# Swapping the row halves of odd heads so that the value products use all four 64x64 tiles of TensorE

## The chip, the cores and the metric

The kernel runs on one core of a Trainium2 chip. The metric is the device time of one execution in microseconds. A core has TensorE (PE in the profile, with its weight loads listed apart as PEld), VectorE (DVE), ScalarE (ACT), GpSimd (POOL) and a queue that issues transfers (SP).

## What is computed

An mLSTM cell over 4 batches x 8 heads (32 heads, called BH), 768 steps and 40 channels, and behind it a feed-forward block over the 3072 tokens. Cut to what matters:

```python
for t in range(S):                       # S = 768, for each of the 32 heads
    m_new = maximum(f_gate[t] + m, i_gate[t])
    f_stab, i_stab = exp(f_gate[t] + m - m_new), exp(i_gate[t] - m_new)
    C = f_stab * C + i_stab * outer(v[t], k[t])        # 40 x 40
    n = f_stab * n + i_stab * k[t]
    y[t] = sigmoid(o_gate[t]) * (C @ q[t]) / maximum(abs(n @ q[t]), 1)
h = y.reshape(3072, 320) @ w_in                        # 320 -> 2048
out = (h * sigmoid(1.702 * h)) @ w_out                 # 2048 -> 320
```

## The kernel before

The 768 steps are cut into six windows `w` of L = 128 steps, for all four batches at once (512 tokens a window). In a window the recurrence is written as attention: within the window a masked 128 x 128 matrix of scores times decay weights is multiplied with the values, and what came before the window enters through a state matrix per head. The normaliser `n` is carried as a column of ones beside the 40 channels of the values (`D1` = 41).

Window 0 is done whole at the start. Windows 1 to 5 are cut in two halves of HL = 64 steps, `x` = 0 and 1. Only the two diagonal 64 x 64 blocks of the scores are then needed; what the first half gives to the second goes through a state in the middle, `state_mid`. All of it is done in two calls `c` = 0 and 1 of 16 heads (PH), eight pairs (NJ) of an even head `i` = 0 and an odd head `i` = 1. For one such window:

- `gates` (DVE) runs two scans over the gates of all heads (rows of 32 partitions) and leaves `st`, 96 rows x 128 steps: rows 0-31 hold the gate term of the keys, rows 32-63 the decay of the queries, rows 64-95 the decay of the values to the end of their half. `m_row` sends the running maximum to memory.
- `spread` fetches `m_row` back, repeated over 64 partitions, into `wt` (steps of keys on partitions, pair, head of the pair, 64 steps of queries).
- `columns` (L288) transposes `st` on PE, so that steps stand on partitions, and the results `cols` are exponentiated by ACT.
- `weights` (L346) makes the decay weights from `wt` and a column of `cols` on ACT, POOL masks them (L350).
- `scores` (L370) multiplies keys with queries in 64 x 64 blocks into the two banks of one PSUM tile, and DVE multiplies the result into `wt` (L373).
- `values` multiplies `wt` with the values (p_o, L411) and the queries with the two states (p_i, L421). DVE adds the two parts (L428, L429), and `outputs` divides and gates.
- `seam` (L438) transposes the result for the feed-forward block, `scale` and `carry` (L464) make the new states.

For a product, the partitions of its two operands name the rows of PE's array, and the partitions of its output name the columns; with 64 on both sides there are four such tiles. In `scores` head `i` stands on rows 64 `i`, and half `x` goes to columns 64 `x`, so all four tiles occur. In `values` the keys' steps are the rows and the queries' steps are the columns, and both come from the same half `x`, so that only the two tiles on the diagonal occur, one bank for each:

```python
for x in range(2):
    t, i = slice(x * HL, x * HL + HL), x ^ flip
    T.matmul(po[t, i, j * D1:(j + 1) * D1], wt[w, c][t, j, i, :], v_st[t, c * PH + 2 * j + i, :],
```

`within(0)` runs the even head of half 0 and the odd head of half 1, then come the products with the states, then `within(1)` the rest.

The order of the work is written out by hand. A window's feed-forward block has an up stage, whose products alternate with DVE, ACT and POOL work and in which the next window's gates, loads and spread are placed, and a down stage of 14 blocks (16 in window 0). `attention` hangs the next window's steps behind given blocks of the down stage: the columns behind block 0, the two calls of `weights` behind 1 and 2, `carry` behind 4, `scores` behind 6, `values` behind 7 and 8, the transposes of `seam` behind 9 and 11 (window 1: 0, 1, 3, 4, 8, 9, 10, 11, 13). Each engine runs its instructions in that order. PSUM tiles of two banks (`banks`: p_cols, p_s, p_o, p_i, p_c, p_x and one of the up stage) share two slots in turn. All transfers go through SP's queue in the order of the program.

Of the kernel before, what the change touches and what calls it, by code (L numbers as in the profile page):

```python
# [26 lines left out]
def kernel(  # L27
# [81 lines left out]
    def load(w, what, bs=slice(0, B)):  # L109
        hs = slice(bs.start * H, bs.stop * H)  # L110
        for c in what:
            if c == "o" and w not in eo:
                eo[w] = ld.tile([L, BH, D], FP, tag="eo", bufs=1, name="eo")
            dst, src = {"k": (k_of(w), k), "q": (q_st, q), "v": (v_st, v), "o": (eo.get(w), o_gate)}[c]
            nc.sync.dma_start(out=dst[:, hs, 0:D],
                              in_=src[bs, :, w * L:(w + 1) * L, :].rearrange("b h s d -> s (b h) d"))

# [80 lines left out]
    for j in range(3):  # L198
        V.tensor_scalar(out=pick[j * BH:(j + 1) * BH, :], in0=ident[0:BH, 0:BH], scalar1=-1.0, scalar2=None,
                        op0=OP.mult)  # L200

    half = const.tile([BH, 2, 64], FP, name="half")
    par = const.tile([BH, 2], FP, name="par")
    pair = const.tile([BH, BH // 2], FP, name="pair")
# [27 lines left out]

    def gates(w):
        m = m_at[w]
        f_run = gate.tile([BH, L], FP, bufs=1, name="f_run")
        m_run = gate.tile([BH, L], FP, bufs=1, name="m_run")
        st = stacked[w] = gate.tile([3 * BH, L], FP, bufs=1, name="st")
        V.tensor_tensor_scan(out=f_run, data0=ones, data1=f_sb[w], initial=0.0, op0=OP.mult, op1=OP.add)
        a = st[0:BH, :]
        V.tensor_tensor(out=a, in0=i_sb[w], in1=f_run, op=OP.subtract)  # L240
        if w == 0:
            room = work.tile([L, H, D1], FP, tag="u", name="room").rearrange("p h d -> p (h d)")
            neg, part = room[0:BH, 0:L], room.bitcast(BF)[0:BH, 2 * L:3 * L]
            V.tensor_tensor(out=neg, in0=f_run, in1=i_sb[w], op=OP.subtract)
            for j in range(3):
                G.tensor_copy(out=part, in_=neg)
                G.tensor_copy(out=a3[j * BH:(j + 1) * BH, :], in_=part)
                if j < 2:
                    G.tensor_tensor(out=neg, in0=neg, in1=part, op=OP.subtract)
        V.tensor_tensor_scan(out=m_run, data0=ones, data1=a, initial=m, op0=OP.mult, op1=OP.max)  # L250
        if w == 0:

            room = work.tile([L, H, D1], FP, tag="u", name="room").rearrange("p h d -> p (h d)")
            left, part = room[0:BH, 0:L], room.bitcast(BF)[0:BH, 2 * L:3 * L]
            for j in range(3):
                rest = left if j else m_run
                V.tensor_copy(out=part, in_=rest)
                V.tensor_copy(out=m3[j * BH:(j + 1) * BH, :], in_=part)
                if j < 2:
                    V.tensor_tensor(out=left, in0=rest, in1=part, op=OP.subtract)  # L260
        else:
            m_row[w] = rows.tile([BH, L], FP, name="m_row")
            nc.sync.dma_start(out=m_row[w], in_=m_run)
        end = m_run[:, L - 1:L]
        if w + 1 < NW:
            m_at[w + 1] = gate.tile([BH, 1], FP, name="m_end")
            V.tensor_tensor(out=m_at[w + 1], in0=f_run[:, L - 1:L], in1=end, op=OP.add)

        mid = m_run[:, HL - 1:HL]
        for x, (old, new) in enumerate(((m, mid), (mid, end)) if w else ((m, end),)):  # L270
            t = slice(x * HL, x * HL + HL) if w else slice(0, L)
            V.tensor_scalar(out=st[BH:2 * BH, t], in0=m_run[:, t], scalar1=old, scalar2=None, op0=OP.subtract)
            V.tensor_scalar(out=st[2 * BH:3 * BH, t], in0=a[:, t], scalar1=new, scalar2=-1.0, op0=OP.subtract,
                            op1=OP.mult)
        if w:
            dec[w] = gate.tile([BH, 2, BH // 2], FP, name="dec")
            both = gate.tile([BH, 2], FP, name="both")
            V.tensor_tensor(out=both[:, 0:1], in0=m, in1=mid, op=OP.subtract)
            V.tensor_tensor(out=both[:, 1:2], in0=mid, in1=end, op=OP.subtract)
            for x in range(2):  # L280
                V.tensor_scalar(out=dec[w][:, x, :], in0=pair, scalar1=both[:, x:x + 1], scalar2=None, op0=OP.mult)

    def banks(name):
        return ps_a.tile([128, 2, 512], FP, tag="a", name=name)

    def columns(w):
        pt = banks("p_cols")[:, 0, :]
        T.transpose(pt[:, 0:3 * BH], stacked[w], ident[0:3 * BH, 0:3 * BH])  # L288
        n = 3 * BH
        if w in dec:  # L290
            n += BH
            T.matmul(pt[:, 3 * BH:n], half.rearrange("p a b -> p (a b)"), dec[w].rearrange("p a b -> p (a b)"),
                     start=True, stop=True)
        c = cols[w] = gate.tile([L, 4 * BH], FP, name="cols")
        V.tensor_copy(out=c[:, 0:BH], in_=pt[:, 0:BH])
# [25 lines left out]
    def spread(w):  # L321

        for c in range(2):
            x = wt[w, c] = work.tile([L, NJ, 2, HL], FP, tag="wt", bufs=2, name="wt")
            for i in range(2):
                src = m_row[w][c * PH:(c + 1) * PH, i * HL:(i + 1) * HL]
                nc.sync.dma_start(out=x[i * HL:(i + 1) * HL].rearrange("s j i t -> s (j i) t"),
                                  in_=src.unsqueeze(0).to_broadcast([HL, PH, HL]))

    def weights(w, c):  # L330
        if w == 0:
# [21 lines left out]
    def scores(w, c):  # L353
        if w == 0:
            pw = [ps_m.tile([L, NP, L], FP, tag="m", name="p_s") for _ in range(2)]
            for p in range(NP):
                for i in range(2):
                    r = slice(i * 64, i * 64 + D)
                    T.matmul(pw[i][:, p, :], kT[w, c][r, p, :], qT[w, c][r, p, :], start=True, stop=True)  # L359
            for i in range(2):  # L360
                V.tensor_tensor(out=wt[w, c][:, :, i, :], in0=pw[i], in1=wt[w, c][:, :, i, :], op=OP.mult)  # L361
            return
        pw = banks("p_s")
        for j in range(NJ):
            b, p = 2 * c + j // NP, j % NP
            for i in range(2):
                r = slice(i * 64, i * 64 + D)
                for x in range(2):
                    t = slice(x * HL, x * HL + HL)
                    T.matmul(pw[t, i, j * HL:(j + 1) * HL], kT[w, b][r, p, t], qT[w, b][r, p, t], start=True,  # L370
                             stop=True)
# [22 lines left out]
    def values(w, c):  # L394
# [9 lines left out]
        hs = slice(c * PH, (c + 1) * PH)  # L404
        po, pi = banks("p_o"), banks("p_i")

        def within(flip):
            for j in range(NJ):
                for x in range(2):
                    t, i = slice(x * HL, x * HL + HL), x ^ flip  # L410
                    T.matmul(po[t, i, j * D1:(j + 1) * D1], wt[w, c][t, j, i, :], v_st[t, c * PH + 2 * j + i, :],  # L411
                             start=True, stop=True)

        within(0)
        for j in range(NJ):
            b, p = 2 * c + j // NP, j % NP
            for i in range(2):
                r = slice(i * 64, i * 64 + D)
                for x, s in enumerate((state[w % 2], state_mid)):
                    t = slice(x * HL, x * HL + HL)  # L420
                    T.matmul(pi[t, i, j * D1:(j + 1) * D1], qT[w, b][r, p, t], s[r, c * NJ + j, :], start=True,  # L421
                             stop=True)
# [34 lines left out]
    def carry(w, c):  # L457
        js = slice(c * NJ, (c + 1) * NJ)
        pc = banks("p_c")
        halves = [slice(0, L)] if w == 0 else [slice(x * HL, x * HL + HL) for x in range(2 if w + 1 < NW else 1)]  # L460
        for j in range(NJ):
            for i in range(2):
                for x, t in enumerate(halves):
                    T.matmul(pc[i * 64:i * 64 + 64, x, j * D1:(j + 1) * D1], k_cols(w, t, c * PH + 2 * j + i),  # L464
                             vw[w, c][t, 2 * j + i, :], start=True, stop=True)
# [4 lines left out]
        for x, dst in enumerate((state_mid, state[1 - w % 2])[:len(halves)]):  # L470
# [346 lines left out]
```

## Time and profile before

| | |
|---|---|
| time, median of 3 runs | 494.53 us (494.53 to 494.54) |
| span of the profile | 492.8 us |
| PE busy | 485.8 us (99%), granted clock 1.000 |
| PEld / DVE / ACT / POOL busy | 394.4 / 343.5 / 194.5 / 149.7 us |
| p_o of windows 1 to 5 (L411) | 640 records, mean 228 ns |
| p_i (L421) | 640 records, mean 228 ns |
| columns (L288) | 6 records, mean 257 ns |
| spread (`wt<-m_row`) | 20 transfers of 256 KB, 6.2 us to landing |
| values (`v_st<-in_v_dram`), keys (`k_st<-in_k_dram`) | 640 KB each, 13.5 and 10.2 us to landing |

A record is one pass of a matmul through the array; a float32 product has two. The mean length of a record says nothing on how fast they follow one another, since many are under way at a time: for that, the chain of waits and the timeline give when a group starts and when the next one does. The chain names a group by line with the time from its start to the start of the next; some records can be missing from a count. "issue" is time in which an engine waited for nothing that the profile shows.

### The profile page before, as it was taken

How to read it: one execution, taken by the hardware profiler on the slowest of the kernel's cores; microseconds unless marked ns; L12 is line 12 of the kernel's file. 1: busy time of each engine (PE TensorE's matmuls, PEld its weight loads, DVE VectorE, ACT ScalarE, POOL GpSimd, SP SyncE). 2: the span in 40 equal slices, each digit the busy share in tenths (PEclk: the TensorE clock that was granted, in tenths of full speed). 3: DMA queues.
4: the chain of work that ended last, by engine and by line, in shares of the span. 5: the costliest groups of instructions: out<-in, count | busy, mean ns of one | idle time of the engine just before them, and what ended most of it. 6: DMA issues, size and time to landing. Idle time of an engine off the chain costs nothing.

```text
span 492.8 us, 11991 instructions
## 1 busy us (share of the span) xinstructions
PE 485.8 (99%) x4996; PEld 394.4 (80%) x4996; DVE 343.5 (70%) x668; ACT 194.5 (39%) x432; POOL 149.7 (30%) x145
## 2 busy tenths in 40 slices
PE   8989999999999999999999999999999999999997
PEld 5764447787777999767999877999876999876997
DVE  5776786977778965768966668967567957353812
ACT  4655558701454801444800354720164630164200
POOL 6020004300497700127610136620045640035300
PEclk9999999999999999999999999999999999999999
DMA  7789997006990000999000899000699000000000
GB/s 164 151 239 180 255 212 177 2 17 118 203 180 4 3 29 3 172 192 127 3 29 3 147 193 151 1 31 3 118 198 171 3 29 3 28 1 1 0 28 27
DMA packets 130342, 44.31 MB, mean 90 GB/s; under 512 B 105168, under 2 KB 127728, under 8 KB 130288
## 3 DMA queue, kind: packets, MB, share of 16 engines
q1 hardware_dynamic: 130288, 43.54, 49.6%
q8 instruction: 39, 0.64, 0.6%
q14 instruction: 15, 0.12, 0.1%
HBM read 39.52 MB, written 4.01 MB: 88 GB/s over the span
## 4 chain that ended last, share of the span: by engine, by line
PE 95%; DVE 3%; POOL 1%; ACT 0%; issue 0%; POOLq 0%; DVEq 0%
PE p_out L658 32%; PE p_h L556 25%; PE p_h L561 8%; PE p_out L607 7%; PE p_h L486 6%; PE p_o L411 4%; PE p_c L464 2%; PE p_s L370 2%; PE p_i L421 2%; PE p_h L492 2%; PE p_x L438 1%; PE p_t L310 1%; PE p_o L401 1%; PE p_s L359 0%; DVE wt L361 0%
## 5 line engine op out<-in xcount | busy, mean ns | idle before, releaser
L598 POOL TENSOR_TENSOR g<-g,parts 128x512 f32<-128x512 f32 x30 | 38.3, 1275 | 128.6 <-DVE parts L590 117.5
L658 PE MATMUL p_out<-w_out_sb,g 128*128 128x160 f32 x480 | 71.0, 302 | 0.0
L658 PEld LDWEIGHTS p_out<-w_out_sb,g 128*128 128x128 f32 x480 | 66.5, 190 | 0.9
L556 PE MATMUL p_h<-xT,w_in_sb 128*128 128x256 f32 x240 | 66.9, 388 | 0.0
L537 ACT ACTIVATE g<-g 128x512 f32<-128x512 f32 x80 | 49.6, 630 | 34.3 <-DVE g L593 25.2
L556 PEld LDWEIGHTS p_h<-xT,w_in_sb 128*128 128x128 f32 x240 | 43.7, 190 | 20.2 <-issue 7.6
L440 ACT COPY xT<-p_x 128x768 f32<-128x768 f32 (+1 forms) x14 | 9.9, 707 | 120.8 <-PE p_x L438 120.8
L663 DVE TENSOR_TENSOR o_sb<-o_sb,p_out 128x160 f32<-128x160 f32 x70 | 21.0, 316 | 46.0 <-PE p_out L658 45.6
L658 PE MATMUL p_out<-t_sb,s 128*128 128x160 f32 x320 | 47.1, 300 | 0.0
L658 PEld LDWEIGHTS p_out<-t_sb,s 128*128 128x128 f32 x320 | 44.4, 190 | 0.2
L589 DVE TENSOR_TENSOR t_x<-p_h,parts 128x256 f32<-128x256 f32 x40 | 16.8, 420 | 39.3 <-PE p_h L561 34.3
L556 PE MATMUL p_h<-t_x,s_in 128*128 128x256 f32 x160 | 41.1, 379 | 0.0
L561 PE MATMUL p_h<-xT,w_in_x 64*128 64x512 f32 x160 | 39.7, 615 | 0.0
L346 ACT ACTIVATE wt<-wt,cols 128x64 f32<-128x64 f32 x160 | 38.8, 343 | 0.0
L392 POOL COPY y<-y 128x128 f32<-128x128 f32 (+1 forms) x14 | 4.0, 285 | 112.3 <-DVE y L389 112.3
L607 PE MATMUL p_out<-w_out_sb,g 128*128 128x320 f32 x128 | 36.5, 438 | 0.0
L556 PEld LDWEIGHTS p_h<-t_x,s_in 128*128 128x128 f32 x160 | 30.4, 190 | 4.1
L586 ACT COPY parts<-p_h 128x256 f32<-128x256 f32 x40 | 14.9, 374 | 46.5 <-PE p_h L556 46.5
L607 PEld LDWEIGHTS p_out<-w_out_sb,g 128*128 128x128 f32 x128 | 23.5, 190 | 9.5 <-DVE w_out_sb L230 0.7
L590 DVE TENSOR_TENSOR parts<-p_h,t_x 128x512 f32<-128x512 f32 x40 | 27.7, 692 | 4.5 <-DVE t_x L589 0.5
L486 PE MATMUL p_h<-xT,w_in_sb 128*128 128x512 f32 x64 | 29.5, 604 | 0.6 <-ACT xT L440 0.6
L597 ACT COPY g<-p_h 128x512 f32<-128x512 f32 x30 | 17.4, 580 | 31.1 <-PE p_h L561 25.7
(183 smaller groups left out, 912.2 us busy)
## 6 DMA issues: line engine op xcount, KB each, us to landing
wt<-m_row SPq DMA_DIRECT2D x20, 256.0 KB, 6.2
k_sq<-in_k_dram SPq DMA_DIRECT2D x16, 320.0 KB, 6.4
q_sq<-in_q_dram SPq DMA_DIRECT2D x16, 320.0 KB, 10.0
out_dram<-o_sb SPq DMA_DIRECT2D x24, 160.0 KB, 1.8
eo<-in_o_gate_dram SPq DMA_DIRECT2D x5, 640.0 KB, 10.1
v_st<-in_v_dram SPq DMA_DIRECT2D x5, 640.0 KB, 13.5
bits<-in_moe_w_in_dram SPq DMA_DIRECT2D x6, 512.0 KB, 5.5
k_st<-in_k_dram SPq DMA_DIRECT2D x4, 640.0 KB, 10.2
```

The costliest lines, as they stand in the source:

```text
L346: A.activation(out=x[:, h, :], in_=x[:, h, :], func=AF.Exp, scale=-1.0, bias=cols[w][:, c * PH + h:c * PH + h + 1])
L411: T.matmul(po[t, i, j * D1:(j + 1) * D1], wt[w, c][t, j, i, :], v_st[t, c * PH + 2 * j + i, :], start=True, stop=True)
L486: T.matmul(ph[j][i], w_in_sb[:, c, f * 128:(f + 1) * 128], x[:, c, :], start=(first and c == 0), stop=(not first and c == 1))
L537: A.activation(out=gs[w, j][:, i, :], in_=gs[w, j][:, i, :], func=AF.Gelu_apprx_sigmoid)
L556: T.matmul(out, a, x[n], start=start, stop=stop)
L561: T.matmul(row, w_in_x[r, j, :], rest_x[r, 2, :], start=not late, stop=late)
L590: V.tensor_tensor(out=y[:, half_w:3 * half_w].rearrange("p (a t) -> p a t", a=2), in0=flat[:, half_w:3 * half_w].rearrange("p (a t) -> p a ...
L597: A.copy(out=g[:, 0, :], in_=row0)
L598: G.tensor_tensor(out=g0, in0=g0, in1=u, op=OP.add)
L607: T.matmul(po, gs[w, f // 2][:, f % 2, b * L:(b + 1) * L], w_out_sb[:, f, :], start=(f == 0), stop=(f == NF - 1))
L658: T.matmul(po, a(f), b[:, f, :], start=(f == 0), stop=(f == NH - 1))
L663: V.tensor_tensor(out=dst, in0=x, in1=po, op=OP.add)
```

## The change

For windows 1 to 5, odd heads keep their keys and values with the two halves of 64 steps exchanged on the partitions: steps 64-127 on partitions 0-63, and steps 0-63 on partitions 64-127. Everything that has keys' steps on partitions follows: the loads of `k` and `v` (three pieces instead of one), `spread` (eight pieces instead of four), the output of `scores`, and `carry`. Even and odd heads of a pair then use different tiles in `values`, and the four products of a pair lie in all four tiles. The even head's products go to bank 0 and the odd head's to bank 1.

The columns for keys and values of odd heads must be exchanged too, while those of the queries stay. `gates` therefore makes a second copy of `st` with its halves exchanged, in a buffer that held `f_run`, and `columns` adds two products: `st` with the identity where the lines of odd heads' key and value terms are zero (`keep`), and the exchanged copy with an identity of only those (`swap`). `keep` and `swap` are made once at the start.

The diff, without the function heads:

```diff
             dst, src = {"k": (k_of(w), k), "q": (q_st, q), "v": (v_st, v), "o": (eo.get(w), o_gate)}[c]
+            if w and c in "kv":
+                for i, t, r in ((0, slice(0, L), slice(0, L)), (1, slice(0, HL), slice(HL, L)),
+                                (1, slice(HL, L), slice(0, HL))):
+                    x = src[:, :, w * L + t.start:w * L + t.stop, :].rearrange("b (p two) s d -> two s (b p) d", two=2)
+                    nc.sync.dma_start(out=dst[r, i::2, 0:D], in_=x[i])
+                continue
...
+    keep, swap = (const.tile([3 * BH, 3 * BH], FP, name=n) for n in ("keep", "swap"))
+    odd = const.tile([3 * BH, 1], FP, name="odd")
+    full = ident[0:3 * BH, 0:3 * BH]
+    V.tensor_reduce(out=odd, in_=full.rearrange("p (j two) -> p two j", two=2)[:, 1], axis=AX.X, op=OP.add)
+    V.tensor_scalar(out=swap, in0=full, scalar1=odd, scalar2=None, op0=OP.mult)
+    V.memset(swap[BH:2 * BH, :], 0.0)
+    V.tensor_tensor(out=keep, in0=full, in1=swap, op=OP.subtract)
...
-        f_run = gate.tile([BH, L], FP, bufs=1, name="f_run")
+        swapped = gate.tile([3 * BH, L], FP, bufs=1, name="f_run")
+        f_run = swapped[0:BH, :]
...
         if w:
+            stacked[w] = st, swapped
+            for x in range(2):
+                V.tensor_copy(out=swapped[:, x * HL:(x + 1) * HL], in_=st[:, (1 - x) * HL:(2 - x) * HL])
...
+    def slot(i, x):
+        return slice((x ^ i) * HL, (x ^ i) * HL + HL)
...
-        T.transpose(pt[:, 0:3 * BH], stacked[w], ident[0:3 * BH, 0:3 * BH])
+        st = stacked[w]
+        if w:
+            T.matmul(pt[:, 0:3 * BH], st[0], keep, start=True, stop=False)
+            T.matmul(pt[:, 0:3 * BH], st[1], swap, start=False, stop=True)
+        else:
+            T.transpose(pt[:, 0:3 * BH], st, full)
...
-                src = m_row[w][c * PH:(c + 1) * PH, i * HL:(i + 1) * HL]
-                nc.sync.dma_start(out=x[i * HL:(i + 1) * HL].rearrange("s j i t -> s (j i) t"),
-                                  in_=src.unsqueeze(0).to_broadcast([HL, PH, HL]))
+                for n in range(2):
+                    src = m_row[w][c * PH + i:(c + 1) * PH:2, n * HL:(n + 1) * HL]
+                    nc.sync.dma_start(out=x[slot(i, n), :, i, :], in_=src.unsqueeze(0).to_broadcast([HL, NJ, HL]))
...
-                    T.matmul(pw[t, i, j * HL:(j + 1) * HL], kT[w, b][r, p, t], qT[w, b][r, p, t], start=True,
-                             stop=True)
+                    T.matmul(pw[slot(i, x), i, j * HL:(j + 1) * HL], kT[w, b][r, p, slot(i, x) if w == 1 else t],
+                             qT[w, b][r, p, t], start=True, stop=True)
...
-        def within(flip):
-            for j in range(NJ):
+        for j in range(NJ):
+            for i in range(2):
                 for x in range(2):
-                    t, i = slice(x * HL, x * HL + HL), x ^ flip
-                    T.matmul(po[t, i, j * D1:(j + 1) * D1], wt[w, c][t, j, i, :], v_st[t, c * PH + 2 * j + i, :],
+                    t, r = slice(x * HL, x * HL + HL), slot(i, x)
+                    T.matmul(po[t, i, j * D1:(j + 1) * D1], wt[w, c][r, j, i, :], v_st[r, c * PH + 2 * j + i, :],
                              start=True, stop=True)
-
-        within(0)
...
-        within(1)
...
-        halves = [slice(0, L)] if w == 0 else [slice(x * HL, x * HL + HL) for x in range(2 if w + 1 < NW else 1)]
+        n = 2 if 0 < w < NW - 1 else 1
         for j in range(NJ):
             for i in range(2):
-                for x, t in enumerate(halves):
+                for x in range(n):
+                    t = slot(i, x) if w else slice(0, L)
                     T.matmul(pc[i * 64:i * 64 + 64, x, j * D1:(j + 1) * D1], k_cols(w, t, c * PH + 2 * j + i),
```

More of the change, by code (lines that the diff above doesn't have):

```diff
@@ L287, in columns @@
         pt = banks("p_cols")[:, 0, :]
-        T.transpose(pt[:, 0:3 * BH], stacked[w], ident[0:3 * BH, 0:3 * BH])
+        st = stacked[w]
+        if w:
+            T.matmul(pt[:, 0:3 * BH], st[0], keep, start=True, stop=False)
+            T.matmul(pt[:, 0:3 * BH], st[1], swap, start=False, stop=True)
+        else:
+            T.transpose(pt[:, 0:3 * BH], st, full)
         n = 3 * BH
@@ L469, in carry @@
             return
-        for x, dst in enumerate((state_mid, state[1 - w % 2])[:len(halves)]):
+        for x, dst in enumerate((state_mid, state[1 - w % 2])[:n]):
             if x:
```

## The prediction

> **What bounds the kernel now.** I read three views in this order: the page's busy shares and its chain, the chain in order of time for one late window, and the timeline around the places that the diff edits.
>
> ```profile
> PE 485.8 (99%) x4996; PEld 394.4 (80%) x4996; DVE 343.5 (70%) x668; ACT 194.5 (39%) x432; POOL 149.7 (30%) x145
> PE 95%; DVE 3%; POOL 1%; ACT 0%; issue 0%; POOLq 0%; DVEq 0%
> ```
>
> PE is busy nearly all the time and carries 95% of the chain that ended last, so a microsecond taken from PE's stream after the first 34 us is a microsecond of the total, as long as nobody else becomes late. The next view, the chain in order of time (start, length, what), tells what PE does per small product:
>
> ```profile
> 22.33 1.71 PE p_o L401 x16
> ...
> 319.38 2.01 PE p_c L464 x128
> ...
> 325.93 2.02 PE p_s L370 x128
> 327.95 2.37 PE p_out L658 x16
> 330.32 0.99 PE p_o L411 x29
> 331.38 0.93 PE p_i L421 x62
> 332.31 0.93 PE p_o L411 x32
> 333.25 2.37 PE p_out L658 x16
> ...
> 395.04 1.99 PE p_c L464 x64
> ```
>
> A float32 product appears as two records. The scores (L370) and the carry (L464) use all four 64x64 tiles: 2.01 / 128 = 15.7 ns a record. One call of `values` is p_o, p_i, p_o, that is 32 + 64 + 32 records; p_i (L421), in four tiles, takes 15 ns, but both halves of p_o (L411), in the two tiles on the diagonal, take 0.93 / 32 = 29 ns. Four tiles or two, one tile gets a record each 58 to 63 ns: the tile, not the issue of instructions, is the limit. The last carry (395.04), with one half of the rows and so two tiles, agrees: 1.99 / 64 = 31 ns. The whole call lasts 333.25 - 330.32 = 2.93 us.
>
> The timeline (start, length, engine, line) gives the places that the diff edits:
>
> ```profile
> 3.08 0.28 DVE L240 TENSOR_TENSOR st<-fi,f_run 32x128 f32<-32x128 f32 x1 [0.18 <-DMA fi<-in_i_gate_dram]
> ...
> 3.84 0.28 POOL L246 CAST room<-room 32x128 bf16<-32x128 f32 x1
> ...
> 296.03 6.95 SPq L327 DMA_DIRECT2D wt<-m_row x4
> ...
> 309.77 0.14 PEld L288 LDWEIGHTS p_cols<-ident,st 96*128 96x128 f32 x1
> ...
> 310.08 0.29 PEld L292 LDWEIGHTS p_cols<-dec,half 32*128 32x128 f32 x2 [0.17 <-issue]
> ...
> 313.68 0.18 DVE L295 COPY cols<-p_cols 128x32 f32<-128x32 f32 x1
> ...
> 314.09 7.74 ACT L346 ACTIVATE wt<-wt,cols 128x64 f32<-128x64 f32 x32
> ...
> 332.39 0.84 DVE L428 TENSOR_TENSOR u<-p_i,cols 128x656 f32<-128x656 f32 x1 [1.71 <-PE p_i L421]
> ...
> 333.34 0.84 DVE L429 TENSOR_TENSOR u<-p_o,u 128x656 f32<-128x656 f32 x1
> ```
>
> Here the reader is to see how late the results are wanted: DVE fetches the columns 3 us after PE made them, ACT wants the spread rows 11 us after their issue ends, and DVE stood idle 1.71 us for the products.
>
> **What the Trainium skill says.** TensorE: Matmul & The Clock Gate, section on LDWEIGHTS, prices a weight load by its columns, P / 1.2 ns, so 53 ns for 64 and 107 ns for 128. The trace agrees: 1.71 us / 16 = 107 ns for L401 with 128 columns, and 58 to 63 ns a tile with 64. TensorEngine Tiling, Key Properties, says that tiles load and multiply independently; L370 and L464 agree. The new p_o breaks a habit of the old code: both row halves write one PSUM bank at a time (rows 0-63 to partitions 0-63, rows 64-127 to partitions 64-127). TensorEngine Tiling, Restrictions and Gotchas, forbids two row tiles in one bank at once; PSUM — Partial Sum Buffer, section on bank collisions, narrows this to one bank and one group of 32 partitions, and lets different column tiles share a bank. By the finer rule the new order is free. No product in the trace before shows such a pair, since each keeps one row half to one bank.
>
> **The change, part by part.**
>
> 1. `values`. Ten calls (five windows, two halves of the heads). After, a call is 64 + 64 records, all in four tiles. The nearest rows are L464, which has p_o's shape (64x64 weights, 41 columns), and L370: 128 records in 2.01 us with their start. So 2.93 - 2.01 = 0.92 us a call, 9.2 us in all. About half of the 32 p_o products still carry a wait for ACT or a DMA, as all 16 of the first half do now; that half is not slower for it (0.99 against 0.93), and the waits per microsecond stay alike. Bounds: 0.5 (waits keep weight loads from being pulled ahead) to 1.0 us a call.
>
> 2. `columns`. For windows 1 to 5 one transpose becomes two float32 products, four records instead of one. Each loads 128 columns, 107 ns from L401; the transposes with 128 columns stand 0.66 / 6 = 110 ns apart (p_x in the chain). So 3 x 0.107 = 0.32 us on PE, five times: +1.6 us. Bounds +1.0 (67 ns a record) and +3.0 (190 ns, PEld's mean, with nothing overlapped). Its readers hide it: the result is ready near 310.5 and DVE takes it at 313.68, behind its queue.
>
> 3. Setup. Four more DVE instructions (reduce, multiply, memset, subtract, on 96 partitions) stand before the first scan. By L205 (0.17), L199 (0.17) and L240 (0.28) they take some 0.7 us; DVE waited about 0.2 us there for the gate's DMA anyway, so L244 moves by 0.55. POOL's L246 needs it, and had been held by two memsets until 3.84, so POOL's chain, which lies on the path here, starts 0.3 to 0.4 late. I take +0.3 us; bounds 0 and +0.7.
>
> 4. Two DVE copies a window in `gates`, some 0.2 us each (L273 with 64 columns takes 0.25). Queued behind them are L589 to L593 for the first up block, which free PSUM that PE wants two blocks on: L593 ends at 282.43, and the tile is wanted near 284.3. Hidden by 1.9 us of slack. The m_row transfer is issued before them.
>
> 5. Transfers. Keys and values go in three pieces instead of one, the spread in eight instead of four; bytes and the 160 and 256 byte runs stay. Later spreads are issued from 296.03 to 302.98, land in 6.2 us (DMA part of the page), and ACT wants them at 314.09: 5 us of slack, and twice as many issues cost less. Hidden. Window 1 is tighter (issued 66.43 to 73.67, wanted at 81.47), but the half wanted first is issued first.
>
> 6. `carry` and `scores` keep four tiles and only change their order (rows 0,0,1,1 and rows 0,1,0,1 run alike today); the last carry keeps two. Nothing.
>
> 7. A wait that gets near. `values` takes two of the two-slot PSUM tiles, and the next call's p_o reuses the slot that L429 frees. L428 now starts some 0.3 us after p_i, the last product: 330.25 + 2.0 + 0.28 = 332.53, and L429 ends near 334.3. PE comes back at 330.25 + 2.0 + 2.37 = 334.62 (before: 335.55, slack 1.4). Likewise the transposes after the second call. Slack 0.1 to 0.3 us, so now and then a stall: +0.4 us, bounds 0 and +3.
>
> Sum: -9.2 + 1.6 + 0.3 + 0.4 = -6.9; 494.53 - 6.9 = 487.6, and since part 1 may bring a little more (p_i's 15 ns), I say 487.4.
>
> **Rivals.**
>
> - PSUM slots become the bound: PE stalls 0.3 us at each of the ten places (five second calls, five transposes behind them). For it: part 7's thin slack. Against: DVE is idle 1.71 us before L428. 494.53 - 9.2 + 1.6 + 0.3 + 3.0 = 490.2.
> - Only half the gain, because waits or the shared bank hold the tiles back: 494.53 - 4.6 + 1.9 = 491.8. Against: the first p_o half has a wait at each product and loses nothing.
> - No gain: the two row halves take turns in the bank, p_o stays at 29 ns, and the added work is left over: 494.53 + 1.6 + 0.3 = 496.4, slower. For it: the coarser of the skill's two rules. Against: the finer one.
> - A better case: the columns and the setup are half hidden and a call saves 1.0: 494.53 - 10 + 1.0 + 0.1 = 485.6.
>
> **How the numbers follow.** Main case 0.64, near 487.4; PSUM slots 0.13; half the gain 0.08; no gain 0.05; better 0.10. The range 485.2 to 490.4 holds the main case, the better one and most of the slots. Faster 0.93, within 0.2% 0.02, slower 0.05.
>
> **What would show it.** Right: p_o and p_i in one run of 128 records near 2.0 us a call; p_cols with four 96*128 records, 0.3 us longer; the first exponentials of the weights 0.3 us later; no wait of PE on DVE's L429. Wrong: p_o records still near 29 ns (bank or waits), PE waiting for DVE before p_o or p_x (slots), ACT waiting for the spread, or PE gaps at the start of the up stages.

## The result, and the profile after

The changed kernel takes 487.65 us (median of 4 runs, 487.55 to 490.55) against 494.53 us (494.53 to 494.56) before: a ratio of 0.9875, with a 95% interval from 0.9838 to 0.9911. In some runs of most kernels here, the one before included, TensorE's granted clock falls to half for some microseconds early in the program, which adds 1.5 us or more; the other runs of the changed kernel lie between 487.55 and 487.70, and below I compare runs at a mean clock of 1.000 (0.999 is counted with it). The profile of after was taken in the run of 490.55 us, so its start is read from another kernel.

Busy times and the chain by engine, from the page of after:

```profile
PE 481.4 (98%) x5011; PEld 389.1 (80%) x5011; DVE 344.8 (71%) x682; ACT 194.6 (40%) x432; POOL 149.9 (31%) x145
...
PE 92%; SPq 5%; DMA 1%; DVE 1%; issue 0%; ACT 0%; DVEq 0%
```

PE is still what bounds the kernel. The 5% of SPq are the lowered clock's: after it the chain goes back through a transfer and SP's queue instead of through PE (at full clock, in `own_bank` below, PE has 94% of the chain and SPq no share). PE has 15 records more, the three more of the columns in each of five windows. The chain in order of time (start, length, what) shows one late window:

```profile
318.69 2.01 PE p_c L490 x128
320.70 4.54 PE p_out L684 x32
325.24 2.03 PE p_s L398 x128
327.27 2.37 PE p_out L684 x16
329.64 1.07 PE p_o L439 x64
330.71 0.93 PE p_i L447 x64
331.64 2.37 PE p_out L684 x16
334.01 1.07 PE p_o L439 x64
```

One call of `values` is p_o and p_i one behind the other, 331.64 - 329.64 = 2.00 us, where it was 2.93. The 64 records of p_o follow each other every 1.07 / 64 = 16.7 ns, not every 29 ns: four tiles are at work. Carry and scores (2.01 and 2.03 us) are as before.

The timeline (start, length, engine, line) at the other places that the diff edits, first three lines of the kernel before that the prediction doesn't show:

```profile
2.19 0.34 DVE L207 COPY half<-par 32x128 f32<-32x128 f32 x1
...
2.49 0.41 DVE L238 TENSOR_TENSOR_SCAN f_run<-one,fi 32x128 f32<-32x128 f32 x1
...
3.29 0.27 DVE L244 TENSOR_TENSOR room<-f_run,fi 32x128 f32<-32x128 f32 x1
```

Then after:

```profile
1.98 0.20 DVE L211 TENSOR_REDUCE odd<-ident 96x1 f32<-96x48 f32 x1
...
2.21 0.30 DVE L212 TENSOR_SCALAR swap<-ident,odd 96x96 f32<-96x96 f32 x1
...
2.77 0.26 DVE L214 TENSOR_TENSOR keep<-ident,swap 96x96 f32<-96x96 f32 x1
...
3.14 0.73 POOL L223 MEMSET q_sq<- 128x768 f32 x1
3.14 0.80 DVE L221 COPY half<-par 32x128 f32<-32x128 f32 x1
3.29 0.66 DVE L253 TENSOR_TENSOR_SCAN f_run<-one,fi 32x128 f32<-32x128 f32 x1
...
4.21 0.27 DVE L259 TENSOR_TENSOR room<-f_run,fi 32x128 f32<-32x128 f32 x1
...
4.54 0.42 POOL L261 CAST room<-room 32x128 bf16<-32x128 f32 x1 [0.68 <-DVE room L259]
...
308.75 0.33 PEld L313 LDWEIGHTS p_cols<-keep,st 96*128 96x128 f32 x2
...
309.00 0.30 PEld L314 LDWEIGHTS p_cols<-swap,f_run 96*128 96x128 f32 x2
...
309.39 0.29 PEld L320 LDWEIGHTS p_cols<-dec,half 32*128 32x128 f32 x2
...
312.65 0.18 DVE L323 COPY cols<-p_cols 128x32 f32<-128x32 f32 x1
...
331.71 0.84 DVE L453 TENSOR_TENSOR u<-p_i,cols 128x656 f32<-128x656 f32 x1 [1.71 <-PE p_i L447]
332.59 0.84 DVE L454 TENSOR_TENSOR u<-p_o,u 128x656 f32<-128x656 f32 x1
```

Three readings. First, the four setup instructions hold DVE from 1.98 to 2.94 us, the subtraction L259 (L244 before) starts at 4.21 instead of 3.29, and POOL, which before came to its cast only behind its own memsets, now waits 0.68 us for it. Second, the columns' two float32 products take 309.39 - 308.75 = 0.64 us of weight loads up to the decay's, where the transpose took 0.31, and DVE still comes for them 3 us later. Third, L454 ends at 333.43, and by the chain PE starts its next p_o at 334.01: 0.58 us in hand, no stall.

On PE, one point recurs in each of the windows 1 to 5: the first up product, a group of 14 records (L556 before) in the chain. Its starts, taken from the chains of several kernels that the experiments below name, divide the gain by stage (us). After is represented by `own_bank`, whose start was not disturbed; from window 1's up stage on, the profile of after itself has the same steps (74.31, 74.16, 74.16, 74.14):

| kernel | first product with fused weights | to window 1's up stage | 1 to 2 | 2 to 3, 3 to 4 | 4 to 5 | to the end |
|---|---|---|---|---|---|---|
| before | 34.09 | 89.69 | 75.82 | 75.66, 75.66 | 75.65 | 66.2 |
| after, in other banks (own_bank) | 34.92 | 87.95 | 74.31 | 74.16, 74.16 | 74.14 | 66.3 |
| only `values` (values_alone) | 34.09 | 87.94 | 73.97 | 73.82, 73.83 | 75.00 | 66.3 |
| after, setup moved (setup_late) | 34.09 | 87.93 | 74.31 | 74.16, 74.16 | 74.15 | 66.2 |

The change gains 1.74 us on the way to window 1's up stage and 6.02 in the four steps from there, and loses 0.83 at the start: -1.74 - 6.02 + 0.83 = -6.9, which is the measured difference. The four tiles alone are worth 1.75 us in the first and 1.84 in each of the later ones.

### The profile page after: what moved, and what is told of

It reads as the page before. It is cut to its first block, busy times and chain, and to the rows that moved or that the text cites. A ratio compares the mean times of both kernels' runs of the same rounds, so it can differ in the third digit from the quotient of the medians.

```text
span 488.8 us, 12119 instructions
## 1 busy us (share of the span) xinstructions
PE 481.4 (98%) x5011; PEld 389.1 (80%) x5011; DVE 344.8 (71%) x682; ACT 194.6 (40%) x432; POOL 149.9 (31%) x145
## 4 chain that ended last, share of the span: by engine, by line
PE 92%; SPq 5%; DMA 1%; DVE 1%; issue 0%; ACT 0%; DVEq 0%
PE p_out L684 32%; PE p_h L582 26%; PE p_h L587 8%; PE p_out L633 7%; PE p_h L512 6%; PE p_c L490 2%; SPq L165 2%; SPq L121 2%; PE p_o L439 2%; PE p_s L398 2%; PE p_i L447 2%; PE p_h L518 2%; PE p_x L463 2%; DMA bits<-in_moe_w_in_dram 1%; PE p_t L338 1%
## 5 line engine op out<-in xcount | busy, mean ns | idle before, releaser
L615 DVE TENSOR_TENSOR t_x<-p_h,parts 128x256 f32<-128x256 f32 x40 | 16.7, 418 | 39.2 <-PE p_h L587 34.6
L512 PE MATMUL p_h<-xT,w_in_sb 128*128 128x512 f32 x64 | 32.1, 647 | 0.6 <-ACT xT L465 0.6
```

Of the source, the lines that this page charges most:

```text
L512: T.matmul(ph[j][i], w_in_sb[:, c, f * 128:(f + 1) * 128], x[:, c, :], start=(first and c == 0), stop=(not first and c == 1))
L615: V.tensor_tensor(out=u2, in0=both[:, 1, right], in1=y[:, left], op=OP.add)
```

## The experiments

Theory: the tile is the limit, four of them give 0.93 us a call, and the setup and the columns are what is given back. Rivals: the order or the bank makes the difference rather than the tiles, the transfers or the readers take part of it, or the cost of setup and columns lies elsewhere.

### Four tiles, or two

`two_tiles` keeps all that the change did, but runs the products of the even heads before and those of the odd heads behind the products with the states, so that at any time p_o has both row halves of one head in one bank, but only two tiles.

```diff
-        for j in range(NJ):
-            for i in range(2):
+        def within(i):
+            for j in range(NJ):
...
+        within(0)
...
+        within(1)
```

> The changed kernel with all its new layouts, loads, columns and setup, but p_o of the even heads runs first, then p_i, then p_o of the odd heads, so that only two tiles are in use during p_o. Theory (one tile gets a record each 60 ns, so the gain is the number of tiles in use): each p_o half is back at 29 ns a record, a call of values at 2.93 us, and the time at 487.6 + 10 x 0.93 = 496.9 us, above the kernel before by the cost of columns and setup. Rival (the gain comes from the new layout, the bank by head or the smaller number of phases, whatever tiles run together): 487 to 489 us. A second reading: here both row halves write one bank at the same time with two tiles; if sharing a bank cost anything, a p_o half would take more than 0.93 us.

Measured: 496.15 us in both runs at full clock (median of all 499.24, ratio 1.0068, interval 1.0034 to 1.0102), 0.75 under the 496.9 expected: the later steps between up stages are 75.9 us, 1.72 more than the changed kernel's and not 2 x 0.93. Its chain in order of time, one call:

```profile
336.47 0.99 PE p_o L439 x29
337.46 0.03 PE p_i L449 x2
337.53 0.88 PE p_i L449 x60
338.43 0.03 PE p_i L449 x2
338.46 0.91 PE p_o L439 x31
339.37 2.37 PE p_out L687 x16
```

The call is 2.90 us, as before the change, with 29 ns a record. The layout, the loads, the setup and the bank by head are those of the changed kernel, so none of them brings the gain; it comes from the products standing in four tiles at a time, and without that the change is a loss of 1.6 us. It shows a second thing: here the two row halves of one head write the same bank in the same stretch, at the pace of two halves that each had their own. That sharing the bank slows them is refuted. In which order they write in it, the profile doesn't tell.

### The bank by itself

`own_bank` exchanges the banks of odd and even heads for the second half of the steps, so that each row half has a bank of its own again, while four tiles stay. Which head a result belongs to is no longer the reference's for that half.

```diff
-                    T.matmul(po[t, i, j * D1:(j + 1) * D1], wt[w, c][r, j, i, :], v_st[r, c * PH + 2 * j + i, :],
+                    T.matmul(po[t, x ^ i, j * D1:(j + 1) * D1], wt[w, c][r, j, i, :], v_st[r, c * PH + 2 * j + i, :],
```

> The changed kernel, but each row half of the array writes to a bank of its own in p_o (bank x ^ i instead of bank i), as every product did before. The halves of even and odd heads are then read in exchanged places by the addition that follows, so this run computes the within-window part of the second 64 steps for the wrong head of each pair; the work is the same. Theory (different column tiles share a bank at no cost): the same time within 0.2%, 487.6 us, p_o 1.07 us. Rival (the shared bank holds p_o at 1.07 us a call where p_i takes 0.93): p_o falls by up to 0.14 us a call, 486.2 us.

Measured: 487.61 and 487.62 us at full clock, the changed kernel's time (median of all 489.92, ratio 0.9881, 0.9821 to 0.9941); p_o takes 1.07 and p_i 0.93 us as there. Sharing the bank costs nothing here. The finer of the skill's two rules (PSUM — Partial Sum Buffer, on bank collisions: different column tiles may write one bank at once) fits both runs; the coarser one (TensorEngine Tiling, Restrictions and Gotchas) doesn't show as a time.

### The products without what they need

`values_alone` is the changed kernel without setup, copies and the columns' second product. The columns of odd heads' keys and values stay with their halves unexchanged.

```diff
-    V.tensor_reduce(out=odd, in_=full.rearrange("p (j two) -> p two j", two=2)[:, 1], axis=AX.X, op=OP.add)
...
-                V.tensor_copy(out=swapped[:, x * HL:(x + 1) * HL], in_=st[:, (1 - x) * HL:(2 - x) * HL])
...
-            T.matmul(pt[:, 0:3 * BH], st[0], keep, start=True, stop=False)
-            T.matmul(pt[:, 0:3 * BH], st[1], swap, start=False, stop=True)
+        T.transpose(pt[:, 0:3 * BH], stacked[w], ident[0:3 * BH, 0:3 * BH])
```

> The changed kernel with one transpose in columns as before, and without keep, swap, odd and the exchanged copy of the gates. It leaves out the exchange of the odd heads' gate columns, so their decays belong to the wrong half; all products, loads and waits else are those of the change. Theory (three terms that add up: -9.3 for the products with values, +1.65 for the columns, +0.84 for the setup): 494.53 - 9.3 = 485.2 us. Rival (columns and setup are hidden, and the products bring only 7 us): 487.6 us. Rival (PE then waits for the two PSUM slots that the value products share): above 486 us with PE waiting for DVE's L429.

Measured: 486.61, 486.62 and 486.65 us at full clock (median of all 486.63, ratio 0.9822, 0.9784 to 0.9859), 1.4 us over the expectation. By the table, the start is back at 34.09, and the distance of two up stages is 73.82, 0.34 below the changed kernel's; 1.2 us are lost between the last two up stages. The chain there:

```profile
399.77 1.13 PE p_i L429 x64
...
404.35 0.62 PE p_i L429 x41
404.97 0.74 issue
405.71 0.56 PE p_i L429 x23
```

In the middle of 64 records PE stands still, and the profile shows no cause; both p_i groups are together 1.2 us longer than 2 x 0.93. Without this pause the time would be some 485.4 (my estimate, 486.6 - 1.2), 0.2 from the expectation. So of the changed kernel's 487.6 some 2.2 us are setup and columns: 0.83 at the start, and 0.34 in each of the four later windows. Window 1 has the columns for nothing (87.95 with them, 87.94 without): the products behind the columns start 0.33 us later with them (79.21 in `setup_late` against 78.88), but two groups of p_out and the scores then take 8.81, 2.35 and 2.03 us instead of 8.98, 2.44 and 2.10, and p_o starts at 103.22 in both. Without them PE's weight loads wait 0.7 us there for the output weights that DVE prepares (`w_out_sb`), with them 0.2.

### The setup at another place

`setup_late` moves the four setup instructions from ahead of the first scan to a place behind window 0's gates, and nothing else.

```diff
-    keep, swap = (const.tile([3 * BH, 3 * BH], FP, name=n) for n in ("keep", "swap"))
...
-    V.tensor_tensor(out=keep, in0=full, in1=swap, op=OP.subtract)
...
     half = const.tile([BH, 2, 64], FP, name="half")
...
+    keep, swap = (const.tile([3 * BH, 3 * BH], FP, name=n) for n in ("keep", "swap"))
...
+    V.tensor_tensor(out=keep, in0=full, in1=swap, op=OP.subtract)
```

> The changed kernel with the four setup instructions on VectorE moved behind the first window's gates, where VectorE is idle until the first scores. Nothing is left out. Theory (the setup delays the first scan and with it the whole start by 0.84 us, all of it on the path): 487.65 - 0.84 = 486.8 us, and the first exponentials of window 0 back at 8.3 us. Rival (the start is set by transfers, and the later start is made up by window 0's end): 487.6 us. If the dip of the granted clock near 34 us in one run of the changed kernel comes from its later start, none is seen here.

Measured: 486.74 to 486.76 us in all four runs (ratio 0.9817, 0.9775 to 0.9859), 0.85 us below the changed kernel, with the first exponentials back at 8.34 and the first product with the fused weights at 34.09. The setup's whole cost was where it stood. None of the four runs has a lowered clock, but the kernel before starts as early and has it in 14 of 37 runs (below), so this doesn't show that the later start is its cause.

### The columns by VectorE instead

`masks_dve` puts the exchange on DVE: the masks become two columns of 96 ones and zeros, for odd and even heads, built late, three instructions make the exchanged `st`, and PE does the single transpose of before.

```diff
+            V.tensor_scalar(out=swapped, in0=st, scalar1=even, scalar2=None, op0=OP.mult)
...
+                V.scalar_tensor_tensor(out=swapped[:, t], in0=st[:, s], scalar=odd, in1=swapped[:, t], op0=OP.mult,
+                                       op1=OP.add)
...
+        T.transpose(pt[:, 0:3 * BH], stacked[w], ident[0:3 * BH, 0:3 * BH])
```

> The changed kernel with the halves of odd heads' gate columns exchanged on VectorE instead of TensorE: two masks of 96 x 1 (built behind the first window's gates, where VectorE is idle), and per window one multiplication of the gates with the even mask and two multiply-adds of the other half with the odd mask, then one transpose in columns as in the kernel before. Nothing is left out. Theory (the two float32 products cost PE 0.335 us in each of the windows 2 to 5, where nothing else waits, and VectorE hides its part behind 1.9 us of slack): 486.75 - 4 x 0.335 = 485.4 us. Rival (VectorE's three instructions of about 0.25 us, queued before the evacuation of the first up block, make PE wait): 486.5 us or more, with a gap of PE at the start of the up stages.

Measured: 485.56 us in the profiled run, where the distance of two up stages is 73.82, that of `values_alone`; the others at full clock took 486.42 and 486.62 (median 486.52, ratio 0.981, 0.9783 to 0.9837). The one instruction more on DVE in `gates` than in the changed kernel is hidden in this profile. But 486.42 and 486.62 are what the rival expects, so they need a cause of their own. Then `masks_again`, the same kernel in a second set of runs:

> The version with the masks on VectorE once more, beside the one with the filled gaps, for the share of runs at a lowered clock: 485.6 to 486.7 us at a clock of 1.000, and by the first theory one run in four or so at 0.996 or lower and 1.5 us or more above that.

486.69 to 486.93 us at full clock (median of all 486.96, ratio 0.9851, 0.9823 to 0.988). Its profile has the 73.82 between up stages too, so the rival's gap is not what costs here. It has the pause of `values_alone` again, 0.47 us of "issue" at 405.33 and another at 400.77; here the p_i groups of the last window took 1.41 and 1.65 us, 1.20 more than 2 x 0.93, and 486.69 - 485.49 is the same 1.20 (485.49 is the version with idle matmuls, below, whose p_i groups took 0.93 each). That the other slower runs have the pause as well is likely, but they have no profile.

`masks_late` moves three more setup instructions (`par`, `pair`, `half`) out of the way of the first scan, to where the masks are built:

```diff
-    V.tensor_reduce(out=par, in_=ident[0:BH, 0:BH].rearrange("p (j two) -> p two j", two=2), axis=AX.X, op=OP.add)
-    V.tensor_reduce(out=pair, in_=ident[0:BH, 0:BH].rearrange("p (j two) -> p j two", two=2), axis=AX.X, op=OP.add)
-    V.tensor_copy(out=half, in_=par.unsqueeze(2).to_broadcast([BH, 2, 64]))
```

> The same with the three older setup instructions for par, pair and half (0.5 us on VectorE before the first scan) also moved behind the first window's gates; they are needed for the columns of window 1 only. Nothing is left out. Theory (the first scan is on the path at the start, but from 3.84 us on POOL's two memsets hold the other half of the chain): between 485.4 and 485.0 us. Rival (the start follows VectorE alone): 484.9 us.

That failed: 487.1 us in the one run at full clock (median of all 488.2, ratio 0.9836, 0.9811 to 0.9862), and in the profile, taken in the run of 488.08 us at a clock of 0.996, the first product with the fused weights starts at 34.12, no earlier. The timeline says why:

```profile
2.58 0.41 DVE L239 TENSOR_TENSOR_SCAN f_run<-one,fi 32x128 f32<-32x128 f32 x1 [0.64 <-DMA fi<-in_f_gate_dram]
```

With DVE's queue empty, the scan waits for the gate's transfer and starts at 2.58, where it started at 2.49 in the kernel before. So the three instructions ahead of it were free where they stood. Of the 488.08 us, 1.70 are the lowered clock (the first eight products with the fused weights take 5.40 us instead of 3.70) and 0.93 the pause in the last window's p_i (1.14 and 1.65 us); what is left, 485.45, is close to the 485.56 of `masks_dve`: the move gains nothing. The run of 487.1 us has no profile.

### The transfers by themselves

`transfers_alone` is the kernel before with keys and values in three pieces and the spread in eight, none of them exchanged.

```diff
+                for n in range(2):
+                    src = m_row[w][c * PH + i:(c + 1) * PH:2, n * HL:(n + 1) * HL]
+                    nc.sync.dma_start(out=x[n * HL:(n + 1) * HL, :, i, :], in_=src.unsqueeze(0).to_broadcast([HL, NJ, HL]))
```

> The kernel before with keys and values of windows 1 to 5 loaded in three pieces and the spread in eight, each to its old place; nothing else is changed and nothing is left out. Theory (twice as many issues on SP are hidden, since the spread lands 5 us before it is wanted): 494.53 us within 0.2%. Rival (a later spread delays the weights on ACT, and with them the scores): above 495.5 us with ACT waiting for the spread.

Measured: 494.53 to 494.55 us at full clock (ratio 1.0003, 0.9986 to 1.0019), and up stages at the places of before within 0.02 us. They are hidden.

### The falling clock

Stretches of 2 us in the profile of after: the stretch and its length, the busy time and instructions of PE, PEld, DVE, ACT and POOL, then the granted clock, the DMA share and GB/s.

```profile
30.00:32.00 2.00, 2.00 (x20) 1.90 (x19) 1.76 (x7) 0.85 (x2) 0.00 (x0) 1.00 0.99 340
32.00:34.00 2.00, 1.10 (x6) 0.55 (x5) 1.57 (x6) 0.48 (x1) 0.50 (x3) 0.90 1.04 314
34.00:36.00 2.00, 1.43 (x4) 0.79 (x4) 0.19 (x1) 1.27 (x3) 2.00 (x2) 0.50 0.64 147
36.00:38.00 2.00, 2.00 (x4) 0.69 (x3) 1.87 (x3) 1.98 (x4) 0.47 (x1) 0.50 0.16 50
```

The clock halves at about 33.6 us, while PE is waiting for DVE ahead of p_x (0.86 us), and stays there to about 40.4; the first eight products with the fused weights then take 6.25 us, in the kernel before 3.70. The kernel before is as idle there (0.67 us of work from 32 to 34 us, in a profile at full clock), and 14 of its 37 runs on three chips had a clock of 0.997 or 0.993, at 1.5 to 3.0 us more. In `masks_busy`, four idle matmuls stand ahead of the last p_x and four ahead of the first product with the fused weights:

```diff
             seam(0, (b - 1) // 2, ((b - 1) % 2,))
+        if b >= 3:
+            keep_busy(4)
```

> This is the version with the masks and the permuted identity on VectorE's side, with four idle matmuls put in before the last transposes of x and four before the first product with the fused weights, so that TensorE has fewer and shorter gaps between 31 and 34 us. Theory: the granted clock falls to 0.50 near 34 us in some runs because TensorE has been mostly idle just ahead of that (0.67 us of work in 2 us); with the gaps filled every run is at a clock of 0.999 or more, and the time is 485.6 us, up to 486.7 in runs that show the pause in p_i. Rival: the lowering doesn't come from those gaps; then some runs show 0.99 to 0.997 as before, at 1.5 to 4.6 us more. If the filling matmuls delay the first product, the start is later by up to 0.3 us and so is the end.

Measured, beside `masks_again` on one chip: 485.48 to 485.49 us in three runs, 486.51 and 486.75 in two, none under a clock of 0.999 (ratio 0.9813, 0.9789 to 0.9836); three of the six runs of `masks_again` were at 0.996 or 0.992. The same stretch in `masks_again` and then in `masks_busy`:

```profile
32.00:34.00 2.00, 0.73 (x5) 0.34 (x3) 0.87 (x3) 0.86 (x3) 1.03 (x2) 1.00 1.06 349
34.00:36.00 2.00, 1.84 (x5) 0.89 (x6) 1.28 (x1) 2.00 (x5) 1.70 (x2) 1.00 0.52 127
```

```profile
32.00:34.00 2.00, 2.00 (x12) 0.93 (x10) 0.82 (x2) 0.90 (x3) 1.08 (x2) 1.00 1.00 351
34.00:36.00 2.00, 2.00 (x7) 0.94 (x6) 1.29 (x2) 2.00 (x5) 1.65 (x2) 1.00 0.82 166
```

The filling delays the first product from 34.16 to 34.41, but the eight then take 3.43 us instead of 3.70, so it costs nothing. Five runs could be chance; two more kernels were to tell:

> The version with the masks on VectorE and the eight idle matmuls once more. Theory: again no run under a clock of 0.999, times 485.5 to 486.8 us. Rival: two or so of the five runs at 0.996 or lower, at 487 us or more.

> This is the changed kernel with nothing but the eight idle matmuls added ahead of the last transposes of x and of the first product with the fused weights. Theory (idle stretches of TensorE between 31 and 34 us let its clock fall): no run has a clock under 0.999, and the time is 487.6 us, as the changed kernel's runs at full clock. Rival (the lowering has another cause, and the five runs of the version with the masks on VectorE had none of it by chance): two or so of the five runs are at 0.996 or lower, 1.5 us or more above that. In the kernel before, on three chips, 14 of 37 runs were.

`masks_busy_b`: 485.44 to 485.50 us in all five runs (median 485.45, ratio 0.9816, 0.9803 to 0.983). But on this fourth chip none of nine runs of the kernel before had a lowered clock either, so this adds nothing on the clock. `after_busy`, the changed kernel with the same filling: 487.62 to 487.83 us in three runs, but 489.24 at a clock of 0.996 in the fourth (median 487.75, ratio 0.9869, 0.9856 to 0.9883), which the theory as I wrote it excludes. That run is the profiled one:

```profile
6.00:8.00 2.00, 0.90 (x8) 0.40 (x7) 1.86 (x7) 1.07 (x2) 1.69 (x6) 1.00 0.96 265
8.00:10.00 2.00, 2.00 (x19) 1.75 (x20) 0.72 (x1) 0.25 (x1) 1.83 (x5) 0.60 1.16 221
10.00:12.00 2.00, 2.00 (x15) 1.67 (x14) 0.00 (x0) 1.38 (x4) 0.00 (x0) 0.55 0.95 258
...
34.00:36.00 2.00, 1.97 (x12) 1.11 (x12) 1.21 (x4) 0.49 (x2) 0.84 (x3) 1.00 0.58 117
```

Near 34 us the clock stays full. It is lowered at another place, from 8 to 12 us, behind another stretch in which PE was idle: 0.90 us of work from 6 to 8, where PE waits for what DVE and POOL make behind the four setup instructions. The profile of `two_tiles`, with the same setup, has the same: 0.82 us of work, then a clock of 0.50. In the profile of the kernel before the stretch from 6 to 8 holds 1.83 us of work, in that of `masks_busy_b` 2.00. So the early setup may cost more than its 0.83 us: it leaves a second idle stretch in which the clock can fall. That fits the lowest clocks on record: 0.988 to 0.990, at 4.6 us more, occur in 5 of the 20 runs of kernels with the early setup (`two_tiles` and `own_bank`) and in no other run. But the idle stretch is not enough by itself: the profile of `own_bank` has 0.85 us of work from 6 to 8 and stays at full clock. Whether it falls differs from run to run, and with four or five runs each I can't give a rate. That filling the stretch ahead of 34 us keeps the clock up rests on none of five runs beside three of six, and is suggested rather than shown.

The Trainium skill (TensorE: Matmul & The Clock Gate, Part 1) describes a gate that grants full or half clock by how busy PE was in a window of some 3.4 us that runs on its own, which is why the same kernel need not meet it twice alike. The half clock and its coming and going between runs agree, and so do the lengths: the falls last 3.41 us in `after_busy` and `masks_late`, 6.83 in after, and 3.41 and 6.83 in `two_tiles`, once or twice that window. The page's rule in its section on HAM oscillation, no idle gap of over about 3.4 us, is too wide here: the longest single gaps ahead of the falls were 0.86 us near 34 and 0.75 near 7.

## Why the prediction was right

The likeliest case came in, and its mechanism is shown: 487.65 measured, 487.4 forecast. Its terms add up to 487.6; the 0.2 us taken off for a faster p_o did not come. By its steps:

1. `values`, forecast -9.2: right. A call fell from 2.93 to 2.00 us, 0.93 against the 0.92 taken, and `two_tiles` shows that it is the tiles, and not the layout, the loads or the bank by head. In the windows 2 to 5 p_o takes 0.14 us more than p_i (1.07 against 0.93), which bounds what the waits of its products cost. The first half of before had as much: it ran from 330.32 to 331.38, 1.06 us, so that the prediction's "not slower" (0.99 against 0.93) was a misreading that cancels in the difference. Only the first call of window 1 is longer, 2.17 us. The 53 ns that the prediction quotes for loading 64 columns is 5 to 10 ns under the trace's 58 to 63 a tile; its sum used the trace.
2. `columns`, forecast +1.6: 1.34, which is 4 x 0.335. The size of one, 0.32 us, was right; their number was wrong. I charged five windows, and window 1 has slack of PE in its down stage that takes it up. The view to ask was the table above, stage by stage, not one late window.
3. Setup, forecast +0.3, bounds 0 and 0.7: 0.83, outside the bounds, and the term that was mis-sized. The four instructions took 0.96 us (I had 0.7). The wait for the gate's DMA took up 0.13 of it, but `half` and the scan behind it became longer (0.80 and 0.66 us instead of 0.34 and 0.41), and since the two overlap, the scan ended 1.05 us late, 0.09 more than the four instructions. So L259 came 0.92 us late and not 0.55. POOL's slack of some 0.3 us was read rightly (0.22 of it was to be had), POOL's cast starts 0.70 late, takes 0.42 us instead of 0.28, and the first product with the fused weights is 0.83 late. `setup_late` gets all of it back. Why `half` grew can be read from the profile of after:

```profile
5.02 0.28 POOL L262 COPY t_sb<-room 32x128 bf16<-32x128 bf16 x1
...
5.16 0.20 DVE L273 COPY t_sb<-room 32x128 bf16<-32x128 bf16 x1
...
6.73 0.41 POOL L264 TENSOR_TENSOR room<-room 32x128 f32<-32x128 f32 x1
6.80 0.40 DVE L273 COPY t_sb<-room 32x128 bf16<-32x128 bf16 x1
```

A copy of DVE that runs beside an instruction of POOL ends 0.06 or 0.07 us behind it, however long it has been: at 5.36 behind 5.30, at 7.20 behind 7.14, and `half` at 3.94 behind the memset of `q_sq`, which ends at 3.87. In before `half` ended at 2.53 behind an instruction of POOL that ended at 2.46, in `masks_late` at 8.49 behind 8.41. So a copy seems to wait for POOL, and the setup pushed `half` from beside an instruction of POOL of 0.29 us to beside a memset of 0.73 us. The scan doesn't wait in this way (in before it ended at 2.90, beside a memset up to 3.21); it ends 0.01 us behind `half`.
4. The copies in `gates`, forecast nothing: right. `masks_dve` with three instructions there has the same 73.82 between up stages as `values_alone` with none.
5. Transfers, forecast nothing: right, by `transfers_alone`. In after a piece of the spread (128 KB instead of 256) lands in 4.4 us instead of 6.2.
6. Carry and scores: right, 2.01 and 2.03 us.
7. The wait for a PSUM slot, forecast +0.4: none in any window. In the timeline's starts, which the sum used, p_o begins at 329.57, and I let DVE start 0.28 us behind 329.57 + 2.00; it starts at 331.71, 0.14 behind. L454 follows 0.88 us later and not 0.95, and ends at 333.43, and the next p_o begins at 333.94: 0.51 us in hand where I saw 0.1 to 0.3.

The sum with the measured terms, -1.75 - 4 x 1.84 + 1.34 + 0.83 = -6.9, is the measured one. Term 3 cost 0.5 us more than forecast, the terms 2 and 7 cost 0.3 and 0.4 less, and that these nearly cancel is luck: the mechanism and the gain of `values` were foreseen, the nearness of the total was not earned. Of the rivals, the slots are refuted by 7, and the half gain and no gain by the 16.7 ns a record and by `own_bank`. The better case did not come. `masks_dve` reaches its 485.6 in one run (485.56), but in another way: it pays neither term 2 nor term 3, while a call still saves 0.93 us. With the filling it took 485.45, the fastest here.

## What to carry to other kernels

Where small products stand in fewer tiles than the array has, count the time of one record for each tile in use; if it is the same with two and with four tiles, moving half of the operands to the other rows nearly halves the time of these products (p_o of a call from about 2.0 to 1.07 us here). What such a move needs (masks, exchanged copies) belongs where an engine has slack: at the start of a kernel even four small instructions of 0.14 to 0.30 us can pass through to the end, and the same four behind the first step cost nothing. Charge an added instruction stage by stage, since one that costs its full length in four windows can be free in the first.

## What was not expected of the hardware

- The granted clock fell to half, for 3.41 or 6.83 us where a profile shows it, in many runs, of the kernel before too, behind stretches in which PE had between 0.7 and 1.1 us of work in 2 us. Other profiles have such stretches at full clock. The losses are near 1.5, 3.0 and 4.6 us, as much as a good edit brings; differences of that size between single runs say nothing until the clock is read.
- A pause of PE in the p_i of the last window, with no cause that the profile shows: 1.2 us in `values_alone` and `masks_again` and 0.93 in `masks_late`, none in `masks_dve`, `masks_busy` and `masks_busy_b`, whose schedule there is the same. All three pauses in a second call come behind record 41 of its 64, though at different times, so they hang on the place in the program. The profile lists transfers of 16 KB on a queue of kind "instruction"; the last of them ahead of the second pause starts at 403.05 us in `values_alone`, 403.45 in `masks_again` and 404.85 in `masks_late`, 1.2 to 1.3 us before that p_i starts, and PE goes on 2.3 to 2.7 us later. In the three profiles without a pause it starts at 401.1 to 401.3, 3.0 to 3.1 us before that p_i. That PE waits for its own instructions would fit, since p_o and p_i are the densest stretch of them, and become denser by the change. It was not tried, and stays open.
- Products of two row halves of the array that go to one PSUM bank in turn, on different partitions, lost nothing: 29 ns a record with two tiles and 16.7 with four, as with separate banks.
- Copies of DVE beside an instruction of POOL ended with it, 0.04 to 0.08 us behind, so that one and the same copy took 0.34 us at one place and 0.80 at another.
